# Finishing the norm of a batch's second token block: the last tokens' squares move to the first units of the expert block ahead

## The chip, the cores and the metric

One Trainium2 chip, one of its cores. The metric is the time of one execution on the device in microseconds (us); lower is better. The inputs are the reference's, float32; all large products are made of two or three float32 matmuls of high and low parts.

## The reference

Attention without softmax in 4 batches of 3008 tokens, gated by u, and then a gated expert layer over all 12032 tokens:

```
scores = (1 / S) * z @ z.T
attn   = maximum(scores, 0) ** 2
x      = u * (attn @ v)                      # 12032 x 256
xn     = x / sqrt(mean(x * x, -1) + 1e-6) * rms_g
g      = xn @ w_gate                         # 256 x 1536
out    = (g * sigmoid(g) * (xn @ w_val)) @ w_out
```

## The kernel before

**Blocks.** The tokens are worked on in 12 blocks of 1024 (NPAIR = 12, three to a batch). Block p has an attention phase A p (24 steps, one to each tile of 128 keys) and an expert phase M p, called expert block p below (12 units, one to each 128 columns of w_gate and w_val). The phases run A0 A1 A2 M0 A3 M1 A4 M2 A5 M3 A6 M4 A7 M5 A8 M6 A9 M7 and so on, then M8 to M11: expert block p comes three attention phases behind its own. Attention blocks are cut by batch (the third of a batch has 960 tokens) and expert blocks are not, so x goes through a tensor in device memory (xg) from the one cut to the other.

**A unit of an expert block** (class Unit, `run`, L885 on) makes seven products of xn's combinations with w (L818, L819 and L820 for each), and between them, for the unit before, the products with w_out (`y`: L846, L847, and L850, which needs the low part hL). ScalarE takes the sums out of PSUM (L825, L902), makes silu (L874, L909) and the high parts hH (L830); VectorE adds and multiplies (L870, L877, L894, L911, L917) and makes the low parts hL (L835). A unit has three places for other work, slots 3f, 3f + 1 and 3f + 2 (`hook`), so a block has 36. Jobs of a slot are issued there in their order on each engine's own queue. In blocks 0, 3, 6 and 9 the third slot stands behind L917 of the unit, ahead of L870 of the next. After the last unit `tail` finishes the block, woven into the first two steps of the next attention phase (L459, L460: scores; L588, L589, L593: the product with v).

**The norm** of block p (`norm_jobs`) consists of jobs: for each half of the tokens squares (ScalarE, L671), their addition (L675), a transpose (L679) and a reduction (L682) on VectorE; then the fold (one small matmul, L698), the guess (L702, L705), a cubic and two Newton steps on 128 x 32 values (L708 to L723), and for each half a transpose back (L727) and two multiplies (L734) that normalize x in place; at last four subtractions (L749). Their results are split into high and low parts in the attention phase A p+2.

Blocks 4 and 7 are treated apart (`is_early`): 960 and 896 of their tokens are ready an attention phase ahead, so eight jobs of squares and sums are done in phase A p+1 (A5, A8). The last 64 or 128 tokens come from the attention phase that ends as expert block p-1 (3 or 6) starts: their gate is in unit 0, they go to xg, and in slot 2 they are loaded into ux (`load_x`, L649). Two jobs work on them: their squares, and their sum (addition, transpose and reduction in one job). Then the other jobs follow, 17 in all.

**Where they go** is decided by a planner. `norm_plan` gives each job an engine, a cost in us and a least distance; `Beside.put` lays a list of jobs in that order into the slots of an expert block:

```
self.room = {
    (e, h): (0.75 if e == "d" else 1.35 if h % 3 == 2 else 0.0)
    for e in "da" for h in range(3 * NF)
}
...
fits = [k for k in open_ if self.room[e, k] >= cost]
h = fits[0] if fits else max(open_, key=lambda k: self.room[e, k])
```

A ScalarE job ("a") may stand only in every third slot; where nothing fits it takes the slot with most room. In expert blocks 3 and 6 `plan_batch` has laid the loads and splits of the next batch's z and v first: two casts of 0.6 (L338 for zst, L362 for vh) in each third slot from 5 to 23, with the low parts of v (vl, L373) on POOL behind them. The scaled z of a later attention phase (L307, L312) stands in slots 32 and 33 without a cost. All DMAs named here are issued on SP's queue.

Of the kernel before, what the change touches and what calls it, by code (L numbers as in the profile page):

```python
# [30 lines left out]
def kernel(  # L31
# [608 lines left out]
    def is_early(p):  # L640
        return p % NP == 1 and 1 < p < NPAIR - 2
# [344 lines left out]
    def norms(p):  # L986
        if ("n", p) not in made:
            made["n", p] = norm_jobs(p)
        return made["n", p]
# [6 lines left out]
    def whole(fn):  # L996
        def go():
            for _ in fn() or ():
                pass
        return go  # L1000

    def norm_plan(p):

        kinds = "addd addd tgggg ddd ddd dddd".replace(" ", "")
        cost = {"a": 1.3, "d": 0.7, "t": 0.0, "g": 0.7}
        if is_early(p):
            kinds = kinds[:8] + "ad" + kinds[8:]
        t = kinds.index("t")
        out = []
        for i, k in enumerate(kinds):  # L1010
            gap = 3 if i == t else 2 if i == t + 1 else 0
            out.append(("a" if k == "a" else "d", cost[k], gap, lambda i=i: whole(norms(p)[i])()))
        return out

    class Beside:
# [70 lines left out]
    def plan_batch(b):  # L1086

        m = beside[(b - 1) * NP]
        soon = 4 if b > 1 else 0
        for c in range(soon):  # L1090
            load, one, two = prep_stat(b, c, what="queries")
            ph = ("A", b * NP - 1)
            at(ph, 3 * c, load)
            at(ph, 3 * c + 3, one)
            at(ph, 3 * c + 4, two)
        todo = [prep_stat(b, c) for c in range(soon, NC)] + [prep_v(b, g) for g in range(NK // 2)]
        done = []
        at(m.phase, 0, lambda: raws["batch"].sort())
        for k, (load, one, two) in enumerate(todo):
            if k == NC - soon and b == 1:  # L1100
                m.put(norm_plan(1)[:8], 3)
            s = max(3 * (k // 2) - 2, 0) + k % 2
            if k >= 6:
                s = max(s, done[k - 6] + 1)
            at(m.phase, s, load)
            dve = k < NC - soon
            h = m.put([("a", 0.6, 0, one), ("d", 0.7 if dve else 0.0, 0, two)], s + (4 if k < 2 else 2))
            done.append(h if dve else h + 1)
# [13 lines left out]
    for i, (e, cost, gap, fn) in enumerate(norm_plan(0)):  # L1122
        g = 28 + i + (2 if i >= 8 else 0) if i < 13 else 48 + i - 13
        at(("A", g // NK), g % NK, fn)
    plan_splits(0, ("A", 2), range(17, 17 + NO))
    at(("A", 2), NK - 1, lambda: load_x(1))
    for p in range(1, NPAIR):
        if p < NPAIR - 2:
            plan_splits(p, ("A", p + 2), range(16, 16 + NO) if p == 1 else range(NO))
        if p == 1:  # L1130
            for i, (e, cost, gap, fn) in enumerate(norm_plan(1)[8:]):
                at(("A", 3), 1 + i, fn)
            continue
        jobs_ = norm_plan(p)
        m = beside[p - 1]
        start = 3 if p == NPAIR - 1 else 5
        if is_early(p):
            at(("A", p + 1), 8, lambda p=p: load_x(p))
            at(m.phase, 2, lambda p=p: load_x(p, True))
            early = 8  # L1140
            for i, (e, cost, gap, fn) in enumerate(jobs_[:early]):
                at(("A", p + 1), 12 + i, fn)
            jobs_ = jobs_[early:]
        else:
            at(m.phase, 0 if p == NPAIR - 1 else 2, lambda p=p: load_x(p))
        h = m.put(jobs_, start)
        if p >= NPAIR - 2:
            for one, two in split_jobs_at(p):
                m.put([("a", 0.6, 0, one), ("d", 0.7, 0, two)], max(h, 15))
# [21 lines left out]
    for c in range(2, NC):  # L1171
        s = 4 * c - 4
# [5 lines left out]
    for g in range(2, NK // 2):  # L1178
        s = 2 * g - 2
# [100 lines left out]
```

## Time and profile before

| | us |
|---|---|
| median of 3 runs | 2036.39 |
| lowest and highest run | 2033.06, 2036.43 |
| the profiled execution | 2035.4 |
| its span | 2033.6 |
| TensorE busy | 2007.7 |
| VectorE busy | 1606.9 |
| ScalarE busy | 1413.0 |
| POOL busy | 226.8 |

The span is the stretch of the profiled execution from its first to its last instruction; the execution's own time is 1.8 us longer. The profile gives each instruction's start and duration, and the idle time of an engine ahead of an instruction with what ended it. TensorE's matmuls are pipelined: a row's duration is longer than the distance to the next row's start, and the distance of the starts is what counts. Idle time of an engine costs nothing unless TensorE or the end waits for it.

### The profile page before, as it was taken

To read this page: it belongs to the slowest core of one execution; us is meant where nothing else is said; L and a number is where in the kernel's file an instruction comes from. 1 tells how busy PE (TensorE), PEld (TensorE's weight loads), DVE (VectorE), ACT (ScalarE), POOL (GpSimd) and SP (SyncE) were. 2 spreads that over 40 slices of the span, in tenths; PEclk is the share of its full clock that TensorE was granted. 3 is DMA by queue.
4 is the path that set the end of the run, shared out by engine and by line. 5 is a ranking of instruction groups with operands and counts; after the bars stand their busy time and mean duration, and the time that the engine had idled before them with its cause. 6 is when DMAs were issued, how large, how long until landed. Compare 5 with 4: busy or idle time off the path is not lost.

```text
span 2033.6 us, 27276 instructions
## 1 busy us (share of the span) xinstructions
PE 2007.7 (99%) x8976; PEld 1673.2 (82%) x8976; DVE 1606.9 (79%) x2699; ACT 1413.0 (69%) x2584; POOL 226.8 (11%) x376
## 2 busy tenths in 40 slices
PE   9999999999999999899999999989999999999999
PEld 7787878888888888788888888878888888888889
DVE  8989978988867876797886786679788678578775
ACT  8888867876766656597676675659757566567665
POOL 0547905000000003100000000310000000000000
PEclk9999999999999999999999999999999999999999
DMA  5135574373484596147347459614734745844343
GB/s 172 48 114 166 135 245 162 140 237 120 127 218 162 153 227 222 65 151 235 133 117 207 169 150 232 213 66 155 230 137 114 206 168 151 202 151 161 127 156 117
DMA packets 355535, 328.38 MB, mean 161 GB/s; under 512 B 222912, under 2 KB 272192, under 8 KB 355392
## 3 DMA queue, kind: packets, MB, share of 16 engines
q1 hardware_dynamic: 355392, 326.64, 53.4%
q8 instruction: 70, 1.15, 0.2%
q14 instruction: 73, 0.60, 0.1%
HBM read 189.73 MB, written 85.72 MB: 135 GB/s over the span
## 4 chain that ended last, share of the span: by engine, by line
PE 89%; DVE 3%; POOL 2%; DMA 2%; issue 2%; ACT 1%; SPq 0%; DVEq 0%; POOLq 0%; ACTq 0%
PE po L588 11%; PE po L589 11%; PE ps L819 11%; PE ps L818 11%; PE ps L820 11%; PE po L593 10%; PE py L850 6%; PE py L846 6%; PE py L847 6%; PE ps L460 3%; PE ps L459 3%; DMA wu<-wc 1%; POOL wolo L143 1%; POOL w L143 1%; POOL ws L143 0%
## 5 line engine op out<-in xcount | busy, mean ns | idle before, releaser
L588 PE MATMUL po<-H,vh 128*128 128x512 f32 (+1 forms) x1152 | 446.6, 388 | 2.3 <-DVE ux L625 0.8
L589 PE MATMUL po<-H,vl 128*128 128x512 f32 (+1 forms) x1152 | 444.9, 386 | 0.0
L825 ACT COPY s<-ps 128x512 f32<-128x512 f32 (+1 forms) x432 | 249.8, 578 | 213.0 <-PE ps L820 212.8
L818 PE MATMUL ps<-xh,wu 128*128 128x512 f32 (+1 forms) x1008 | 389.1, 386 | 0.4 <-ACT s L825 0.4
L819 PE MATMUL ps<-xh,wu 128*128 128x512 f32 (+1 forms) x1008 | 388.2, 385 | 0.8 <-DMA wu<-wc 0.6
L820 PE MATMUL ps<-xl,wu 128*128 128x512 f32 (+1 forms) x1008 | 387.7, 385 | 0.0
L593 PE MATMUL po<-L,vh 128*128 128x512 f32 (+1 forms) x1104 | 336.6, 386 | 3.4 <-DVE L L511 3.2
L830 ACT CAST hH<-s 128x512 fp32r<-128x512 f32 (+1 forms) x288 | 176.7, 614 | 194.8 <-DVE s L917 187.6
L835 DVE TENSOR_TENSOR hL<-s,hH 128x512 fp32r<-128x512 f32 (+1 forms) x288 | 200.5, 696 | 104.6 <-ACT hH L830 93.0
L471 ACT ACTIVATE r<-ps 128x512 f32<-128x512 f32 x354 | 195.9, 595 | 105.0 <-PE ps L460 87.1
L588 PEld LDWEIGHTS po<-H,vh 128*128 128x128 f32 x1152 | 216.3, 188 | 47.7 <-ACT H L498 2.3
L589 PEld LDWEIGHTS po<-H,vl 128*128 128x128 f32 x1152 | 216.5, 188 | 40.1
L478 DVE TENSOR_TENSOR r<-ps,r 128x512 f32<-128x512 f32 (+1 forms) x287 | 186.5, 681 | 73.3 <-ACT r L471 72.8
L593 PEld LDWEIGHTS po<-L,vh 128*128 128x128 f32 x1104 | 206.4, 188 | 45.8 <-DVE L L511 7.0
L511 DVE TENSOR_TENSOR L<-r,H 128x512 fp32r<-128x512 f32 (+1 forms) x334 | 226.8, 712 | 9.7 <-ACT r L505 7.5
L846 PE MATMUL py<-hH,woh 128*128 128x512 f32 (+1 forms) x576 | 222.5, 386 | 0.3 <-ACT hH L830 0.3
L847 PE MATMUL py<-hH,wol 128*128 128x512 f32 (+1 forms) x576 | 222.0, 385 | 0.0
L818 PEld LDWEIGHTS ps<-xh,wu 128*128 128x128 f32 x1008 | 189.2, 188 | 38.1 <-ACT s L825 1.8
L819 PEld LDWEIGHTS ps<-xh,wu 128*128 128x128 f32 x1008 | 189.2, 188 | 38.0 <-DMA wu<-wc 2.7
L820 PEld LDWEIGHTS ps<-xl,wu 128*128 128x128 f32 x1008 | 189.2, 188 | 36.1
L850 PE MATMUL py<-hL,woh 128*128 128x512 f32 (+1 forms) x576 | 176.3, 387 | 12.8 <-DVE hL L835 12.8
L373 POOL TENSOR_TENSOR vl<-raw,vh 128x128 fp32r<-128x128 f32 x144 | 78.0, 581 | 942.3 <-ACT vh L362 942.3
(96 smaller groups left out, 2979.3 us busy)
## 6 DMA issues: line engine op xcount, KB each, us to landing
wu<-wc SPq DMA_DIRECT2D x288, 448.0 KB, 4.0
kept<-halves SPq DMA_DIRECT2D x168, 256.0 KB, 2.1
raw<-in_v SPq DMA_DIRECT2D x44, 256.0 KB, 4.0
out_T<-y SPq DMA_DIRECT2D x44, 256.0 KB, 2.0
raw<-in_zT SPq DMA_DIRECT2D x38, 256.0 KB, 4.4
u<-in_uT SPq DMA_DIRECT2D x36, 256.0 KB, 4.2
ux<-xg SPq DMA_DIRECT2D x16, 512.0 KB, 4.3
wc<-wohi SPq DMA_DIRECT2D x21, 256.0 KB, 2.5
```

The costliest lines, as they stand in the source:

```text
L511: nc.vector.tensor_tensor(lo[:, :n], a[:, :n], f32(hi[:, :n]), op=ALU.subtract)
L588: nc.tensor.matmul(po[d][:, :n], wh[:, j, ds], hi[:, :n], start=(i == 0), stop=False)
L589: nc.tensor.matmul(po[d][:, :n], wl[:, j, ds], hi[:, :n], start=False, stop=(ends and lo is None))
L593: nc.tensor.matmul(po[d][:, :n], wh[:, j, ds], lo[:, :n], start=False, stop=ends)
L818: nc.tensor.matmul(ps[:, :n], wh[:, o, :], xh[:, :n], start=start, stop=False, skip_group_check=True)
L819: nc.tensor.matmul(ps[:, :n], wl[:, o, :], xh[:, :n], start=False, stop=False, skip_group_check=True)
L820: nc.tensor.matmul(ps[:, :n], wh[:, o, :], xl[:, :n], start=False, stop=stop, skip_group_check=True)
L825: nc.scalar.copy(s, ps[:, :self.n])
L835: nc.vector.tensor_tensor(lo[:, :self.n], s, f32(self.h[h][0][:, :self.n]), op=ALU.subtract)
L846: nc.tensor.matmul(acc[h, d][:, :n], woh[:, f, ds], hi[:, :n], start=(f == 0), stop=False)
L847: nc.tensor.matmul(acc[h, d][:, :n], wol[:, f, ds], hi[:, :n], start=False, stop=False)
L850: nc.tensor.matmul(acc[h, d][:, :n], woh[:, f, ds], lo[:, :n], start=False, stop=(f == NF - 1))
```

## The change

In `norm_plan` the two jobs on the last tokens of blocks 4 and 7 get letters of their own, "r" (squares, ScalarE, cost 0.1) and "s" (sum, VectorE, cost 0.4), in place of "a" (1.3) and "d" (0.7). Nothing else differs.

```
         if is_early(p):
-            kinds = kinds[:8] + "ad" + kinds[8:]
+            kinds = kinds[:8] + "rs" + kinds[8:]
+        cost.update(r=0.1, s=0.4)
...
-            out.append(("a" if k == "a" else "d", cost[k], gap, lambda i=i: whole(norms(p)[i])()))
+            out.append(("a" if k in "ar" else "d", cost[k], gap, lambda i=i: whole(norms(p)[i])()))
```

With it the planner lays the 17 jobs into other slots of expert blocks 3 and 6 (the same in both):

| job | slot before | slot now |
|---|---|---|
| squares of the last tokens | 26 | 5 |
| their sum | 27 | 8 |
| fold | 30 | 11 |
| guess, cubic | 32, 33 | 13, 14 |
| two Newton steps | 34, 35 | 15, 16 |
| transpose back, two multiplies (first half) | 35, 35, 35 | 17, 18, 19 |
| the same (second half) | 35, 35, 35 | 20, 21, 22 |
| four subtractions | 35, 35, 35, 35 | 23, 24, 25, 26 |

On VectorE, at the end of expert block 3, the last jobs of slot 35 stood before ahead of L870, which belongs to the last unit (misc, qt, ux and xc are the norm's tiles, s and hL the unit's):

```order
L727 STREAM_TRANSPOSE qt<-misc 128x512
L734 SCALAR_TENSOR_TENSOR ux_7865<-ux_7865,front,qt 128x512
L734 SCALAR_TENSOR_TENSOR ux_7867<-ux_7867,front,qt 128x512
L749 TENSOR_TENSOR xc<-ux_7865 128x512
L749 TENSOR_TENSOR xc<-ux_7867,xc 128x512
L749 TENSOR_TENSOR ux_7865<-ux_7867,ux_7865 128x512
L749 TENSOR_TENSOR xc<-ux_7867,xc 128x512
L870 TENSOR_TENSOR s<-ps,s 128x512
L835 TENSOR_TENSOR hL<-s,hH 128x512
```

Now the same place reads:

```order
L835 TENSOR_TENSOR hL<-s,hH 128x512
L911 TENSOR_TENSOR s<-s 128x512
L917 TENSOR_TENSOR s<-ps,s 128x512
L870 TENSOR_TENSOR s<-ps,s 128x512
L835 TENSOR_TENSOR hL<-s,hH 128x512
L877 TENSOR_TENSOR s<-s 128x512
```

The eleven jobs of slot 35 are gone from between L917 and L870. On VectorE in unit 6 of expert block 3, where only the unit's own instructions stood, there is now one norm step in each of the three slots:

```order
L727 STREAM_TRANSPOSE qt<-misc 128x512
L870 TENSOR_TENSOR s<-ps,s 128x512
L835 TENSOR_TENSOR hL<-s,hH 128x512
L894 TENSOR_TENSOR s<-ps,s 128x512
L877 TENSOR_TENSOR s<-s 128x512
L734 SCALAR_TENSOR_TENSOR ux_7865<-ux_7865,front,qt 128x512
L835 TENSOR_TENSOR hL<-s,hH 128x512
L734 SCALAR_TENSOR_TENSOR ux_7867<-ux_7867,front,qt 128x512
L911 TENSOR_TENSOR s<-s 128x512
L917 TENSOR_TENSOR s<-ps,s 128x512
```

A step stands ahead of L870, one ahead of the second L835 and one ahead of L911. On ScalarE, at the end of unit 1 of expert block 3 (slot 5), there stood before:

```order
L909 ACTIVATE s<-s 128x512
L338 CAST zst_8370<-raw 128x512
L338 CAST zst_8372<-raw 128x512
L830 CAST hH<-s 128x512
L825 COPY s<-ps 128x512
```

and now:

```order
L909 ACTIVATE s<-s 128x512
L338 CAST zst_8370<-raw 128x512
L338 CAST zst_8372<-raw 128x512
L671 ACTIVATE q_8376<-ux_7865 128x64
L671 ACTIVATE q_8377<-ux_7867 128x64
L830 CAST hH<-s 128x512
```

The two squares of 64 columns stand behind the two zst casts, ahead of the next unit's first hH.

## Rows read from the trace of the kernel before

**Rows 1.** The page, part 1: busy us, share of the span and count by engine.

```profile
PE 2007.7 (99%) x8976; PEld 1673.2 (82%) x8976; DVE 1606.9 (79%) x2699; ACT 1413.0 (69%) x2584; POOL 226.8 (11%) x376
```

**Rows 2.** Timeline of TensorE, end of expert block 3 (start, us, instruction, [idle before]).

```profile
855.58 0.39 PE L847 MATMUL py<-hH,wol 128*128 128x512 f32 x1
862.37 1.22 PE L850 MATMUL py<-hL,woh 128*128 128x512 f32 x2 [6.40 <-DVE hL L835]
...
865.74 0.39 PE L846 MATMUL py<-hH,woh 128*128 128x512 f32 x1
```

**Rows 3.** Timeline of TensorE, end of expert block 6.

```profile
1362.05 0.39 PE L847 MATMUL py<-hH,wol 128*128 128x512 f32 x1
1368.84 1.22 PE L850 MATMUL py<-hL,woh 128*128 128x512 f32 x2 [6.41 <-DVE hL L835]
...
1374.10 0.40 PE L459 MATMUL ps<-mh,zst 128*128 128x512 f32 x1
```

**Rows 4.** Timeline of TensorE, end of expert block 4 and start of attention phase 7.

```profile
1037.92 0.61 PE L850 MATMUL py<-hL,woh 128*128 128x512 f32 x2
...
1039.73 0.39 PE L846 MATMUL py<-hH,woh 128*128 128x512 f32 x1
...
1040.64 0.39 PE L459 MATMUL ps<-mh,zst 128*128 128x512 f32 x1
...
1041.55 0.39 PE L588 MATMUL po<-H,vh 128*128 128x512 f32 x1
```

**Rows 5.** Windows: blocks 3, 4, end of 3 (length, busy (x) by engine, PEclk, DMA, GB/s).

```profile
771.00:846.00 75.00, 75.00 (x334) 62.23 (x333) 51.42 (x80) 51.75 (x97) 25.86 (x48) 1.00 0.51 170
953.00:1028.00 75.00, 75.00 (x334) 62.10 (x333) 60.27 (x104) 46.10 (x85) 0.00 (x0) 1.00 0.50 159
...
850.00:880.00 30.00, 23.60 (x98) 19.10 (x97) 28.59 (x54) 19.66 (x35) 0.00 (x0) 0.89 0.25 93
```

**Rows 6.** Timeline of VectorE, end of expert block 3.

```profile
853.08 0.68 DVE L917 TENSOR_TENSOR s<-ps,s 128x512 f32<-128x512 f32 x1
...
860.43 0.68 DVE L749 TENSOR_TENSOR xc<-ux,xc 128x512 f32<-128x512 f32 x1
861.03 0.68 DVE L870 TENSOR_TENSOR s<-ps,s 128x512 f32<-128x512 f32 x1
```

**Rows 7.** Timeline of ScalarE in expert block 3: behind slot 5, and slot 26.

```profile
777.88 0.63 ACT L830 CAST hH<-s 128x512 fp32r<-128x512 f32 x1 [0.64 <-DVE s L917]
...
828.47 0.39 ACT L671 ACTIVATE q<-ux 128x64 f32<-128x64 f32 x2
```

**Rows 8.** Tile ux, 755 to 790: loads of the last tokens (ns; first, last start).

```profile
L649 SPq DMA_DIRECT2D ux<-xg x2: 377/419/461, 772.0 to 772.5; - x2
...
DMA to landing us min/median/max: 2.5/2.8/3.0
```

**Rows 9.** VectorE by line and form, expert block 4, 962 to 1004 (busy us, mean ns).

```profile
L835 DVE TENSOR_TENSOR hL<-s,hH 128x512 fp32r<-128x512 f32 x11 | 7.6, 693 | 5.0 <-ACT hH L830 4.6
...
L734 DVE SCALAR_TENSOR_TENSOR ux<-ux,front,qt 128x512 f32<-128x512 f32 x2 | 1.5, 745 | 0.0
...
L721 DVE SCALAR_TENSOR_TENSOR misc<-misc 128x32 f32<-128x32 f32 x2 | 0.4, 193 | 0.1
```

**Rows 10.** VectorE by line and form, expert block 3, 784 to 826 (last: idle before).

```profile
L835 DVE TENSOR_TENSOR hL<-s,hH 128x512 fp32r<-128x512 f32 x11 | 9.2, 840 | 4.9 <-ACT hH L830 4.4
...
L917 DVE TENSOR_TENSOR s<-ps,s 128x512 f32<-128x512 f32 x6 | 4.2, 692 | 4.5 <-PE ps L820 4.5
...
L911 DVE TENSOR_TENSOR s<-s 128x512 f32<-128x512 f32 x5 | 3.5, 693 | 4.1 <-ACT s L825 4.1
```

**Rows 11.** Timeline of expert block 0, units 10 and 11.

```profile
348.19 0.94 DVE L312 SCALAR_TENSOR_TENSOR ml<-raw,mh 128x512 fp32r<-128x512 f32 x1 [0.36 <-POOL vl L373]
...
352.70 0.61 PE L850 MATMUL py<-hL,woh 128*128 128x512 f32 x2
...
353.30 0.50 PE L818 MATMUL ps<-xh,wu 128*128 128x512 f32 x1
```

## The prediction

> **What bounds the kernel now.** I read the page first: TensorE is busy 99% of the span, VectorE 79%, ScalarE 69% [rows 1]. A step on VectorE or ScalarE therefore counts only where TensorE stands still for it. So I looked for holes in TensorE's row at the places that the change touches, the expert blocks 3 and 6 (their slots are shared with the loads of a new batch, and the norms of blocks 4 and 7 are finished in them).
>
> The timeline of TensorE at the end of expert block 3 has a hole [rows 2]: a matmul of L847 starts at 855.58, the next one, of L850, only at 862.37, and 6.40 us of it are put down to VectorE's hL (L835). Behind it the matmuls are slow: that pair of L850 shows 1.22 us, the same pair at the end of block 4 0.61 [rows 4]. The end of block 6 is the same picture [rows 3]: 1362.05, then 1368.84. Block 4 is the twin without it [rows 4]: the same sequence of lines in one beat, 0.23 us a matmul (four from 1040.64 to 1041.55), on into attention phase 7. The granted clock tells the slow matmuls: a mean of 0.89 in the 30 us around the first hole, 1.00 in the stretches of blocks 3 and 4 ahead of it [rows 5]. TensorE had just stood still for 6.40 us, and then ran at the lower level (1.2 GHz) for a while.
>
> What VectorE did in the hole stands in [rows 6]: after L917 at 853.08 it worked without a pause through norm steps, the last a subtraction (L749) at 860.43. Only then comes L870 at 861.03, which ScalarE's silu and so the rest of the last unit needs, and behind it L835, for which TensorE waits. That is the heap in the last slot: of the 17 jobs of this plan 11 stand in slot 35.
>
> **The change part by part, and what each costs.** It adds and removes no instruction and moves no DMA; only places change. Two costs fall: squares from 1.3 to 0.1, their sum from 0.7 to 0.4. With room 1.35 in each third slot, two casts of 0.6 leave 0.15; so squares at 1.3 waited for the first slot without casts (26), and squares at 0.1 fit slot 5. All steps behind follow: sum 8, fold 11, Newton steps from 13, multiplies 18 to 22, subtractions 23 to 26.
>
> *Slot 35 is emptied.* Block 3: the hole, 862.37 - 855.58 = 6.79, less the 0.23 of the beat, 6.56 us. Then the slow stretch: from that L850 to the L846 at 865.74 3.37 us, in the twin (1037.92 to 1039.73) 1.81: 1.56. Together 8.12 [rows 2, 4]. Block 6: 1368.84 - 1362.05 - 0.23 = 6.56; from there to the L459 at 1374.10 5.26, in the twin (1037.92 to 1040.64) 2.72: 2.54. Together 9.10 [rows 3, 4]. **Sum 17.2 us.** The slow stretch goes with the hole, since TensorE then doesn't stand still before it. What is late next is what is late in block 4, and there nothing is.
>
> *The squares in slot 5* [rows 7]. Behind two zst casts ScalarE waits 0.64 us for VectorE's L917 before its cast at 777.88. The two squares of 64 columns took 0.39 us together where they stood, at 828.47. They fit into the 0.64 and cost nothing. Block 7's have 128 columns, some tenths more; if they ran over, the cast behind them would be late by that, and only the matmuls of its result, further down the unit, could feel it. The squares now need the late part of x early: its two loads are issued at 772.0 and 772.5 and land 2.5 to 3.0 us later [rows 8], at 775.5 at the latest, and the squares can't start before 777.88 - 0.64 = 777.24. Margin 1.7 us; the loads and their place in SP's queue are unchanged. Cost 0, at the upper end what a late load takes beyond that.
>
> *The norm steps, one to a slot, in units 2 to 8.* Block 4 does just this: VectorE is busy 60.27 us in 75 and TensorE 75.00 of 75.00 [rows 5]. Block 3 had 51.42 there, TensorE 75.00 as well. The steps that move cost VectorE, at block 4's durations [rows 9], at most ten large ones at 0.75 (two transposes, four multiplies, four subtractions) and sixteen small ones at 0.19 (thirteen of 32 columns, and the three of the sum): 10.6 us per block, into seven units. VectorE's idle time in the 42 us from 784 on was 4.9 + 4.5 + 4.1 = 13.5 us [rows 10], so there is room.
>
> What block 4 lacks is POOL: in block 3 it is busy 25.86 us with vl, block 4 0.00 [rows 5]. Beside it VectorE is slower: L835 takes 840 ns on average [rows 10] against 693 in block 4 [rows 9]. The nearest row for a step like the moved ones is in block 0, beside the same POOL work [rows 11]: L312, a multiply with two inputs, waited 0.36 us behind POOL and took 0.94, 0.2 more than such a multiply in block 4. About eight of the large moved steps with two inputs fall beside POOL in a block. Ends: 0, if VectorE's idle time takes it all, and 8 x (0.36 + 0.2) = 4.5 us per block if all of it came onto TensorE. I take 0.25 us per block, 0.5 in both, near the lower end: that unit of block 0 held up TensorE by some 0.15 us (the pair at 352.70, one beat for each, makes the next due at 353.15; it starts at 353.30) [rows 11].
>
> The Trainium skill, "SBUF — State Buffer", section "Who interferes with whom", speaks against this change: a VectorE instruction with two SBUF inputs and a GpSimd instruction that reads SBUF lock each other out, and the later one blocks until the other is done. By it the sum would hold the upper end, 9.0 us for both blocks, wherever no idle time of VectorE stands behind a blocked step.
>
> *The fold* (one matmul, a fourth PSUM tile) goes from slot 30 to slot 11. Block 4 has it in slot 14, within the stretch in which TensorE is busy 75.00 of 75.00 [rows 5]: 0.
>
> **Sum.** -17.2 + 0.5 = -16.7 us. The profiled execution took 2035.4 us (span 2033.6), 1.0 under the median of the three runs, 2036.39. Forecast 2035.4 - 16.7 = **2018.7 us**.
>
> **The rivals.**
> 1. *VectorE beside POOL holds TensorE up, but less than the heap did.* For it: the slower L835 [rows 10] and the blocked L312 [rows 11]. Against it: 13.5 us of idle time, and block 0, where POOL and extra steps meet at almost no loss. At the upper end: 2035.4 - 17.2 + 9.0 = 2027.2. Chance 0.10.
> 2. *The stall only moves.* Attention phase 6 might be waiting for something else that the 8 us hid (a load, a late score). Against it: phase 7 behind block 4 starts in the beat [rows 4], and no turned tile is due among phase 6's first steps. 2035.4. Chance 0.04.
> 3. *Slower: VectorE becomes the bound in units 2 to 8.* Place: the step that now stands between L917 and L870, ahead of the chain to hL. If VectorE had no idle time to give, the 10.6 us of moved steps would come onto the path in both blocks, 21.2, and the lock-outs, 9.0, with them: 30.2 - 17.2 = +13.0, 2048.4. It decides from the point where a unit's steps and lock-outs (three at 0.75 and three at 0.56, 3.9 at most) exceed VectorE's idle time in a unit (33 matmuls of one beat, 7.5 us; 13.5 us in 42 are 2.4 in 7.5), in most units and not in the two or three that hold three large ones. Chance 0.03.
> That the steps are not moved is no rival: the order of the instructions shows them moved.
>
> **How the numbers follow.** Forecast 0.83, rivals 0.10, 0.04, 0.03. No change means within 0.2%, some 4 us, about what a measurement here can tell. Forecast and rival 1 are faster by more: 0.93; rival 2 is the same: 0.04; rival 3 slower: 0.03. Range: the lowest run shown (2033.06) less 17.2, and 1.4 for a run lower still, gives 2014.5; upwards the median less 16.7 is 2019.7, and rival 1 up to near its end takes it to 2025.5.
>
> **What would show it.** Right: no hole over 0.5 us at the ends of blocks 3 and 6, pairs of L850 at 0.61 us and a granted clock of 1.00 there, the span some 17 us shorter, VectorE near 61 us in the 75 us window of block 3. Wrong: TensorE waits for hL or for a PSUM tile inside units 5 to 8 (rivals 1 and 3), a ScalarE wait for ux in unit 1, or a new hole in the first steps of attention phase 6 or 9 (rival 2).

## The result and the profile after

Four runs of the changed kernel took 2016.62 to 2019.02 us, median 2016.85; four of the kernel before 2032.38 to 2036.43, median 2034.72. The ratio is 0.9915, 95% interval 0.9898 to 0.9932: faster by 0.85%. The profiled execution is the slowest of the four (2019.02 us, span 2017.2 against 2033.6), so the two traces differ by 16.4 us, where 16.7 were forecast (2018.7).

In the windows of [rows 5] VectorE has the moved work in block 3 now, and the stretch that held the hole has TensorE busy in all of its 30 us at a clock of 1.00 (columns as there):

```profile
771.00:846.00 75.00, 75.00 (x332) 61.75 (x331) 59.03 (x101) 52.00 (x97) 24.92 (x48) 1.00 0.50 167
...
850.00:880.00 30.00, 30.00 (x134) 24.85 (x133) 28.30 (x48) 27.85 (x49) 0.00 (x0) 1.00 0.39 139
```

The place of [rows 2] in TensorE's timeline, the end of block 3:

```profile
855.15 0.39 PE L847 MATMUL py<-hH,wol 128*128 128x512 f32 x1
855.38 0.62 PE L850 MATMUL py<-hL,woh 128*128 128x512 f32 x2
...
857.19 0.39 PE L846 MATMUL py<-hH,woh 128*128 128x512 f32 x1
```

From L847 to L850 it takes 0.23 us instead of 6.79, and from there to the L846 1.81 instead of 3.37: the twin's numbers [rows 4], 8.12 us back. At the end of block 6 [rows 3] it is 0.23 and 2.72 as well (1354.91 to 1357.63), 9.10 back:

```profile
1354.68 0.39 PE L847 MATMUL py<-hH,wol 128*128 128x512 f32 x1
1354.91 0.62 PE L850 MATMUL py<-hL,woh 128*128 128x512 f32 x2
...
1357.63 0.39 PE L459 MATMUL ps<-mh,zst 128*128 128x512 f32 x1
```

What was given back lies in unit 5 of the same blocks. TensorE's timeline there, in block 3:

```profile
803.05 0.61 PE L850 MATMUL py<-hL,woh 128*128 128x512 f32 x2
803.50 0.48 PE L818 MATMUL ps<-xh,wu 128*128 128x512 f32 x1
803.82 0.40 PE L819 MATMUL ps<-xh,wu 128*128 128x512 f32 x1
...
805.77 0.50 PE L818 MATMUL ps<-xh,wu 128*128 128x512 f32 x1
806.11 0.39 PE L819 MATMUL ps<-xh,wu 128*128 128x512 f32 x1
```

From the pair of L850 to the second L819 are twelve matmuls, 2.72 us in the beat; here it is 3.06, and in block 6 too (1302.60 to 1305.66). The missing 0.34 us stand ahead of and behind two L818, which write a PSUM tile that ScalarE must have read before. VectorE's timeline ahead of it shows where the lateness begins, in the cubic step of slot 14:

```profile
799.62 0.39 DVE L708 TENSOR_TENSOR misc<-misc 128x32 f32<-128x32 f32 x1
800.04 0.39 DVE L710 TENSOR_TENSOR misc<-misc 128x32 f32<-128x32 f32 x1
...
801.30 0.39 DVE L716 SCALAR_TENSOR_TENSOR misc<-misc 128x32 f32<-128x32 f32 x1
801.61 0.68 DVE L870 TENSOR_TENSOR s<-ps,s 128x512 f32<-128x512 f32 x1
```

Five instructions on 32 columns take 0.39 us each, 2.0 us together, ahead of L870, where each takes 0.19 in block 4. They start 0.42 us apart, and POOL was at eight subtractions meanwhile, one each 0.42 us:

```profile
798.66 3.40 POOL L373 TENSOR_TENSOR vl<-raw,vh 128x128 fp32r<-128x128 f32 x8 [3.46 <-ACT vh L362]
```

VectorE by line and form, 784 to 826 (busy us, mean ns, idle before):

```profile
L835 DVE TENSOR_TENSOR hL<-s,hH 128x512 fp32r<-128x512 f32 x11 | 8.3, 752 | 2.0 <-ACT hH L830 1.9
...
L734 DVE SCALAR_TENSOR_TENSOR ux<-ux,front,qt 128x512 f32<-128x512 f32 x4 | 3.2, 793 | 0.0
...
L675 DVE TENSOR_TENSOR q<-q,q 128x64 f32<-128x64 f32 x1 | 0.4, 422 | 0.0
...
L679 DVE STREAM_TRANSPOSE q<-q 128x64 f32<-128x64 f32 x1 | 0.2, 248 | 0.0
```

The four multiplies rose from 745 [rows 9] to 793 ns on average. But only one of them met POOL's subtracting (806.84 to 811.15), and that one took 0.95 us; the others took 0.74 to 0.75:

```profile
810.75 0.95 DVE L734 SCALAR_TENSOR_TENSOR ux<-ux,front,qt 128x512 f32<-128x512 f32 x1
```

Of the subtractions (L749) two met POOL, and took 0.74 and 0.94 us instead of 0.68 to 0.69. VectorE's idle time ahead of L835 fell from 4.9 [rows 10] to 2.0 us: it paid for the steps, and TensorE for no more than the 0.34 us above.

The squares in slot 5 went where they were expected. ScalarE's timeline, and then the loads of the last tokens (tile ux: start of the issues; time to landing):

```profile
775.26 1.13 ACT L338 CAST zst<-raw 128x512 fp32r<-128x512 f32 x2
776.29 0.40 ACT L671 ACTIVATE q<-ux 128x64 f32<-128x64 f32 x2
777.02 0.62 ACT L830 CAST hH<-s 128x512 fp32r<-128x512 f32 x1 [0.34 <-DVE s L917]
```

```profile
L649 SPq DMA_DIRECT2D ux<-xg x2: 376/416/456, 771.1 to 771.7; - x2
...
DMA to landing us min/median/max: 2.6/3.0/3.4
```

ScalarE still waits 0.34 of its 0.64 us [rows 7] for L917 behind them. The loads had landed by 771.7 + 3.4 = 775.1, 1.2 us ahead.

### The profile page after: what moved, and what is told of

Read it like the earlier page. It is cut to its first block, busy times and chain, and to the rows that moved or that the text cites. A ratio compares the mean times of both kernels' runs of the same rounds, so it can differ in the third digit from the quotient of the medians.

```text
span 2017.2 us, 27280 instructions
## 1 busy us (share of the span) xinstructions
PE 2004.2 (99%) x8976; PEld 1670.2 (83%) x8976; DVE 1605.6 (80%) x2699; ACT 1414.7 (70%) x2584; POOL 224.4 (11%) x376
## 4 chain that ended last, share of the span: by engine, by line
PE 92%; DMA 3%; DVE 2%; issue 1%; POOL 1%; ACT 1%; SPq 0%; DVEq 0%; POOLq 0%; ACTq 0%
PE po L588 11%; PE po L589 11%; PE ps L818 11%; PE ps L819 11%; PE ps L820 11%; PE po L593 11%; PE py L846 6%; PE py L847 6%; PE py L850 6%; PE ps L460 4%; PE ps L459 4%; DMA wu<-wc 1%; POOL w L143 1%; DMA T<-diag 1%; POOL wolo L143 1%
## 5 line engine op out<-in xcount | busy, mean ns | idle before, releaser
L818 PE MATMUL ps<-xh,wu 128*128 128x512 f32 (+1 forms) x1008 | 389.8, 387 | 0.5 <-ACT s L825 0.4
L819 PE MATMUL ps<-xh,wu 128*128 128x512 f32 (+1 forms) x1008 | 388.2, 385 | 1.3 <-DMA wu<-wc 1.1
L835 DVE TENSOR_TENSOR hL<-s,hH 128x512 fp32r<-128x512 f32 (+1 forms) x288 | 199.1, 691 | 98.1 <-ACT hH L830 87.3
L818 PEld LDWEIGHTS ps<-xh,wu 128*128 128x128 f32 x1008 | 189.2, 188 | 39.6 <-ACT s L825 3.0
L846 PE MATMUL py<-hH,woh 128*128 128x512 f32 (+1 forms) x576 | 221.7, 385 | 0.3 <-ACT hH L830 0.3
L847 PE MATMUL py<-hH,wol 128*128 128x512 f32 (+1 forms) x576 | 221.5, 385 | 0.0
L819 PEld LDWEIGHTS ps<-xh,wu 128*128 128x128 f32 x1008 | 189.3, 188 | 38.0 <-DMA wu<-wc 2.7
L850 PE MATMUL py<-hL,woh 128*128 128x512 f32 (+1 forms) x576 | 174.8, 385 | 0.0
```

Source lines behind the costliest of these rows:

```text
L818: nc.tensor.matmul(ps[:, :n], wh[:, o, :], xh[:, :n], start=start, stop=False, skip_group_check=True)
L819: nc.tensor.matmul(ps[:, :n], wl[:, o, :], xh[:, :n], start=False, stop=False, skip_group_check=True)
L835: nc.vector.tensor_tensor(lo[:, :self.n], s, f32(self.h[h][0][:, :self.n]), op=ALU.subtract)
L846: nc.tensor.matmul(acc[h, d][:, :n], woh[:, f, ds], hi[:, :n], start=(f == 0), stop=False)
L847: nc.tensor.matmul(acc[h, d][:, :n], wol[:, f, ds], hi[:, :n], start=False, stop=False)
L850: nc.tensor.matmul(acc[h, d][:, :n], woh[:, f, ds], lo[:, :n], start=False, stop=(f == NF - 1))
```

## The experiments

The theory: each block's heap in slot 35 stood by itself ahead of L870 of the last unit, and its emptying is the gain. Rivals: one cause for both blocks; that the norm is finished early; that another part of the heap counted. For the small loss in unit 5: POOL beside the large steps, POOL beside the small ones, or the place itself. In the experiments the 17 jobs get slots by hand (in the first one those of block 7 alone), in the order of the change's table; the changed kernel's are

```
[5, 8, 11, 13, 14, 15, 16, 17, 18, 19, 20, 21, 22, 23, 24, 25, 26]
```

and the edit is

```
             jobs_ = jobs_[early:]
+            for (e, cost, gap, fn), h in zip(jobs_, SLOTS):
+                at(m.phase, h, fn)
+            jobs_ = []
```

**One block only.** The old slots for block 7 alone:

```
+            if p == 7:
+                SLOTS = [26, 27, 30, 32, 33, 34] + [35] * 11
```

> The jobs of block 4 (in expert block 3) keep the new slots, those of block 7 (in expert block 6) go back to the old ones. If each block's heap in slot 35 costs by itself, expert block 3 shows no hole and expert block 6 its hole of 6.4 us with the slow matmuls behind it: half the gain, 2034.7 - 7.7 = 2027.0 us, ratio 0.996. If the gain has one common cause (a state of the chip, a chain that both blocks share), it is there whole or not at all: 2017 or 2034.7 us.

Measured: 2026.34 us against 2035.28, ratio 0.9956 (0.9941 to 0.9971). In the trace the end of block 3 is whole (the window of [rows 5]), and block 6 has the hole with the slow pair behind it, in TensorE's timeline:

```profile
850.00:880.00 30.00, 30.00 (x134) 24.86 (x133) 28.30 (x48) 27.85 (x50) 0.00 (x0) 1.00 0.37 130
```

```profile
1354.13 0.39 PE L847 MATMUL py<-hH,wol 128*128 128x512 f32 x1
1360.91 1.22 PE L850 MATMUL py<-hL,woh 128*128 128x512 f32 x2 [6.39 <-DVE hL L835]
```

The two blocks count singly; a common cause is out.

**Late, but one to a slot.**

```
-SLOTS = [5, 8, 11, 13, 14, 15, 16, 17, 18, 19, 20, 21, 22, 23, 24, 25, 26]
+SLOTS = [14, 17, 20, 22, 23, 24, 25, 26, 27, 28, 29, 30, 31, 32, 33, 34, 35]
```

> All 17 jobs one to a slot, but late: squares in slot 14, sum 17, fold 20, guess 22, then one to a slot up to the last subtraction in slot 35. If the heap was the cost, the time is that of the changed kernel, 2016.9 us within 1, because one subtraction of 0.6 us in slot 35 is less than the 0.8 us that the old heap had free (7.35 us of steps made a hole of 6.56). If what counts is that the norm is finished early (something behind it waits for its result), much of the gain is gone: 2025 us or more, with a wait at the start of attention phase 6.

Measured: 2019.29 us (2018.19 to 2020.79), ratio 0.9919 (0.9903 to 0.9936): nearly all of the gain, with the norm finished where it was before. "Within 1" was too narrow: there is no hole in the block, but VectorE has no idle time in the last unit and carries its lateness on, into the first steps of attention phase 6. TensorE's timeline there:

```profile
862.29 0.39 PE L589 MATMUL po<-H,vl 128*128 128x512 f32 x1
863.02 0.50 PE L588 MATMUL po<-H,vh 128*128 128x512 f32 x1 [0.34 <-DVE y L861]
```

0.73 instead of 0.23 us, behind VectorE's copy of y. Early slots are worth about that, one to a slot is worth the rest.

**Four subtractions left in slot 35.**

```
-SLOTS = [5, 8, 11, 13, 14, 15, 16, 17, 18, 19, 20, 21, 22, 23, 24, 25, 26]
+SLOTS = [5, 8, 11, 13, 14, 15, 16, 17, 18, 19, 20, 21, 22, 35, 35, 35, 35]
```

> The new slots, but the four subtractions stay together in slot 35. They take VectorE 4 x 0.6 = 2.4 us; less the 0.8 us that are free there, a hole of 1.6 us at the end of expert blocks 3 and 6, so 2016.9 + 3.2 = 2020.1 us. If a hole of this length also lowers the clock behind it, about 1.5 us more in each block: 2023 us. If the multiplies and transposes, or the number of jobs, made the old hole, there is none: 2016.9 us.

Measured: 2022.4 us (2021.01 to 2027.44), ratio 0.9941 (0.9926 to 0.9956). TensorE's timeline at the end of block 3 and in attention phase 6:

```profile
857.11 0.39 PE L847 MATMUL py<-hH,wol 128*128 128x512 f32 x1
858.22 0.73 PE L850 MATMUL py<-hL,woh 128*128 128x512 f32 x2 [0.73 <-DVE hL L835]
...
864.58 0.50 PE L588 MATMUL po<-H,vh 128*128 128x512 f32 x1 [0.55 <-DVE y L861]
```

A hole of 0.88 us over the beat, not 1.6, and a second one some six us later in the attention phase, which the expectation did not have: what the first hides isn't gone, VectorE is still late. Together they cost 1.80 us in block 3 (857.11 to 864.58, against 855.15 to 860.82 for the same matmuls in the changed kernel), near the 1.6 expected. The granted clock stayed at 1.00 in these 30 us; no slow matmuls follow. The median is higher than two such blocks make it; in the profiled run 2.0 us of the difference stand there before block 3 begins (a matmul at 772.94, the same one at 770.94 in the changed kernel) and so don't come from the heap. A heap of subtractions alone makes a hole, then, and a smaller heap a smaller one; the transposes and multiplies are not needed for it.

**The cubic step in slot 16.**

```
-SLOTS = [5, 8, 11, 13, 14, 15, 16, 17, 18, 19, 20, 21, 22, 23, 24, 25, 26]
+SLOTS = [5, 8, 11, 13, 16, 18, 19, 20, 21, 22, 23, 24, 25, 26, 27, 28, 29]
```

> As the changed kernel, but the cubic step (five instructions on 128 x 32) goes from slot 14, the third slot of unit 4 and beside the start of POOL's work, to slot 16, the second slot of unit 5; all steps behind move on by two or three slots. If the small waits of TensorE in unit 5 of expert blocks 3 and 6 (0.2 and 0.3 us ahead of L818) come from these five, each of which takes 0.39 instead of 0.19 us beside POOL, they are gone and the five take 0.19 each: 0.5 us less in all, 2016.4 us, which only the trace can tell. If they come from the large steps with two inputs, the waits stay.

Measured: 2017.83 us (2017.48 to 2018.35), ratio 0.9914 (0.9899 to 0.9929), which can't be told from the changed kernel's. The trace can. VectorE, and TensorE over the same twelve matmuls:

```profile
804.82 0.18 DVE L708 TENSOR_TENSOR misc<-misc 128x32 f32<-128x32 f32 x1
...
805.71 0.19 DVE L716 SCALAR_TENSOR_TENSOR misc<-misc 128x32 f32<-128x32 f32 x1
```

```profile
803.72 0.61 PE L850 MATMUL py<-hL,woh 128*128 128x512 f32 x2
...
806.44 0.39 PE L819 MATMUL ps<-xh,wu 128*128 128x512 f32 x1
```

2.72 us: the waits are gone, and the five take 0.19 each behind POOL's work. One large moved step with two inputs meets POOL's subtracting here too (a multiply at 825.95, 0.94 us), and TensorE shows no wait for it. By its trace this is the best of the versions, by some tenths of a us in each block; the times are too near to show it.

**POOL writes and doesn't read.** The slots are those of the changed kernel, given by hand; only vl's filling differs:

```
-nc.gpsimd.tensor_tensor(lo[:, a, c], tiles["raw"][:, a, c], f32(hi[:, a, c]), op=ALU.subtract)
+nc.gpsimd.memset(f32(lo[:, a, c]), 0.0)
```

> The changed kernel, but POOL fills vl of the batches 1 to 3 with zeros (as many instructions, which write and don't read) instead of subtracting: the low part of v is left out there. If the five small cubic instructions in slot 14 take 0.39 us because POOL reads beside them, they take 0.19 us now, L835 falls from 0.84 to about 0.69 us, and the small waits ahead of L818 in unit 5 are gone, with slots unchanged. If it is POOL's presence or its writes, or slot 14 itself, they stay.

Measured: one run, 2019.19 us. With the cubic in slot 14, as in the changed kernel, VectorE and TensorE in block 3:

```profile
800.07 0.18 DVE L708 TENSOR_TENSOR misc<-misc 128x32 f32<-128x32 f32 x1
...
800.96 0.19 DVE L716 SCALAR_TENSOR_TENSOR misc<-misc 128x32 f32<-128x32 f32 x1
```

```profile
803.50 0.62 PE L850 MATMUL py<-hL,woh 128*128 128x512 f32 x2
...
806.22 0.39 PE L819 MATMUL ps<-xh,wu 128*128 128x512 f32 x1
```

0.19 each, L835 at 0.68 on average, and 2.72 us without a wait: it is POOL's subtracting that stretches them, not the slot. That it is the reading in it this run does not show on the small steps. The memsets take no input and so wait for no cast of vh; the last before unit 5 were over by 775.5, and POOL had nothing to do beside the cubic step. They met one large step with two inputs, L835 in unit 0, which took no longer for it (POOL, then VectorE):

```profile
773.62 1.83 POOL L373 MEMSET vl<- 128x128 f32 x12 [11.43 <-PE po L589]
```

```profile
773.86 0.69 DVE L835 TENSOR_TENSOR hL<-s,hH 128x512 fp32r<-128x512 f32 x1 [0.89 <-ACT hH L830]
```

So for a large step writing alone is shown to cost nothing, for a small one it was not tried.

**The squares in slot 2.**

```
-SLOTS = [5, 8, 11, 13, 14, 15, 16, 17, 18, 19, 20, 21, 22, 23, 24, 25, 26]
+SLOTS = [2, 8, 11, 13, 14, 15, 16, 17, 18, 19, 20, 21, 22, 23, 24, 25, 26]
```

> Only the squares of the last tokens go from slot 5 to slot 2, the slot in which their loads are issued. If the squares wait for the landing (some 3 us behind the issue, about 6 us behind ScalarE's arrival there), ScalarE stands about 6 us at the end of unit 0, and TensorE, with 1 to 2 us of slack behind it, 3 to 5 us in each block: 2023 to 2027 us. If the landing isn't what bounds how early they can come, 2016.9 us.

Measured: 2032.41 us against 2036.22, ratio 0.9981 (0.9971 to 0.9990): nearly all of the gain lost, more than expected. ScalarE and TensorE at the end of unit 0 of block 3:

```profile
776.03 0.26 ACT L671 ACTIVATE q<-ux 128x64 f32<-128x64 f32 x1 [5.71 <-DMA ux<-xg]
```

```profile
773.55 0.39 PE L820 MATMUL ps<-xl,wu 128*128 128x512 f32 x1
778.18 0.50 PE L818 MATMUL ps<-xh,wu 128*128 128x512 f32 x1 [4.24 <-ACT s L825]
...
781.42 0.63 PE L819 MATMUL ps<-xh,wu 128*128 128x512 f32 x1
```

ScalarE stands 5.71 us as expected, and TensorE 4.63 - 0.23 = 4.4. The expectation left out that the matmuls behind such a stand are slow (0.63 us, the lower level of the clock, as in [rows 2]): between the same matmuls block 3 takes 6.1 us more than in the changed kernel (773.55 to 782.91, against 771.17 to 774.44). So the landing of the last tokens is what bounds how early the squares can come, and slot 5 is the first place behind it.

**Eleven small instructions in slot 14.** Both Newton steps join the cubic one:

```
-SLOTS = [5, 8, 11, 13, 14, 15, 16, 17, 18, 19, 20, 21, 22, 23, 24, 25, 26]
+SLOTS = [5, 8, 11, 13, 14, 14, 14, 17, 18, 19, 20, 21, 22, 23, 24, 25, 26]
```

> As the changed kernel, but both Newton steps join the cubic one in slot 14: eleven small instructions ahead of L870 of unit 5, beside POOL. If each waits for a POOL instruction (one each 0.42 us), they take 4.6 us for as long as POOL runs, 2.6 us more than the five, and TensorE's loss in unit 5 grows from 0.3 to over 2 us in each block: 2021 us or more. If small instructions cost only their 0.22 us, it is 2.4 us in all and the loss grows by some tenths: 2017.5 us.

Measured: 2022.31 us (two runs), ratio 0.9933 (0.9913 to 0.9952), an interval that takes in the changed kernel's 0.9915; the trace has to tell them apart. VectorE, and TensorE over the twelve matmuls:

```profile
800.72 0.39 DVE L708 TENSOR_TENSOR misc<-misc 128x32 f32<-128x32 f32 x1
...
802.82 0.38 DVE L719 TENSOR_TENSOR misc<-misc 128x32 f32<-128x32 f32 x1
803.24 0.19 DVE L721 SCALAR_TENSOR_TENSOR misc<-misc 128x32 f32<-128x32 f32 x1
...
804.25 0.68 DVE L870 TENSOR_TENSOR s<-ps,s 128x512 f32<-128x512 f32 x1
```

```profile
804.15 0.61 PE L850 MATMUL py<-hL,woh 128*128 128x512 f32 x2
806.12 0.50 PE L818 MATMUL ps<-xh,wu 128*128 128x512 f32 x1 [1.36 <-ACT s L825]
...
808.75 0.39 PE L819 MATMUL ps<-xh,wu 128*128 128x512 f32 x1
```

The first six go at POOL's pace, 0.42 us from one to the next; then POOL's eight subtractions are through and the rest go at 0.22. Together 3.5 us instead of 4.6, and TensorE loses 4.60 - 2.72 = 1.88 us.

**The same eleven with vl at zero** (both edits above):

> The same eleven in slot 14, with vl filled with zeros as above (the low part of v of the batches 1 to 3 is left out). If POOL's reading is what stretches them, the eleven take 2.4 us and most of the loss in unit 5 is gone; if it is the heap of eleven alone, the loss is that of the eleven beside the subtracting POOL.

Measured: one run, 2019.64 us. TensorE over the twelve matmuls:

```profile
805.52 0.61 PE L850 MATMUL py<-hL,woh 128*128 128x512 f32 x2
...
808.95 0.39 PE L819 MATMUL ps<-xh,wu 128*128 128x512 f32 x1
```

3.43 us, a loss of 0.71. So of the 1.88 us some 1.2 come from POOL's subtracting (here, too, the memsets were over before) and 0.7 from eleven instructions in one place.

## Why the prediction was right

**The sum.** The hole and the slow matmuls behind it went in both blocks, to the hundredth of a us what the twin in block 4 had given (8.12 and 9.10). The one-block and the four-subtractions runs show the mechanism: a heap counts singly by block and by the time it takes. That nothing else waits in its place (rival 2) is shown by the 30.00 of 30.00 us behind block 3, and behind block 6 by the L459 at 1357.63, on time; the late and the four-subtractions runs show what such a wait looks like when VectorE is late by 1 to 2 us.

**The loss beside POOL** was taken at 0.25 us a block and measures 0.34 in block 3's unit 5. The step that failed is its working, and the near agreement is luck: the prediction charged the lock-out to eight large steps with two inputs and let the small ones count 0.19 us each. In block 3 only three of the large moved steps met POOL (one multiply, two subtractions). They lost 0.06 to 0.26 us each, and TensorE's row shows no loss there. The five small ones doubled, since each waits for one of POOL's instructions whatever its own length, and they stood together ahead of L870. The cubic in slot 16 and vl at zero take the loss away. The rule of the Trainium skill ("SBUF — State Buffer", "Who interferes with whom") holds here in its kind: L675 with two inputs took 0.42 us beside POOL, 0.22 with vl at zero, and L679 with one took 0.25 in both. The same section of the Trainium skill exempts a GpSimd instruction that only writes; the memsets beside L835 agree (0.69 us), and no run here shows it on a small step. L712, a tensor_scalar with one input, was stretched too (0.38 us at 800.47); the Trainium skill counts tensor_scalar there among the operations that can take the shared ports, when its operands meet the conditions. Rival 1's upper end was far off because few large steps met POOL, and because VectorE's idle time took the rest, as the prediction argued from [rows 10].

**The squares.** No cost, as forecast; the margin ahead of them was 1.2 us instead of 1.7, the landing being up to 0.4 us slower. The run with slot 2 shows that the margin is needed.

**Rival 3** would have needed VectorE without idle time. It was busy 59.03 of 75 us, near the 61 forecast.

17.2 less twice 0.34 is 16.5 us, against 16.4 between the two spans. That it comes out to a tenth is partly luck, for two differences outside of blocks 3 and 6 cancel in it. The changed run is 0.85 us ahead before block 3 begins (a matmul at 770.04, the same one at 770.89 before). And at the start of expert block 5 it loses 1.0 us more than the run before, mostly to a wait for a load of w:

```profile
1103.81 0.50 PE L819 MATMUL ps<-xh,wu 128*128 128x512 f32 x1 [0.58 <-DMA wu<-wc]
```

The medians differ by 17.9: the profiled execution of the changed kernel was 2.2 us above its median. The wait for w may be a part of that; no other run of this kernel has a trace to show it.

## What to carry to other kernels

When a planner's fallback puts what doesn't fit into the last slot, look there first: a list of small jobs that each hide anywhere can cost their whole length when they stand together ahead of one instruction that the bounding engine waits for. Price such a heap by the start-to-start distance in the bounding engine's row against a twin stage without it, slow matmuls behind the hole included. And beside a POOL that subtracts, count the VectorE instructions that meet it, not their elements: a step of 32 columns lost 0.20 us here, a multiply of 512 columns 0.20 as well.

## What had not been expected

VectorE and a POOL that subtracts take turns one instruction at a time: small VectorE instructions of 0.19 us go at 0.42 us each, the pace of POOL's 128 x 128 subtractions, for as long as those last. And a hole that is partly hidden shows again: with four subtractions left (2.4 us of work) TensorE lost 0.88 us at the heap and 0.70 at a second place some six us later (863.65 to 864.58, less the beat), since VectorE had no idle time to make it good in between. Behind the stand of 0.9 us the granted clock stayed at 1.00; behind 4.4 and 6.6 us matmuls of 0.63 us followed.
